# An attention and highway kernel: single PSUM banks for the first batches, paired output halves copied after both are written, x pairs of batches 3 and 4 moved ahead

## The chip, the cores and the metric

The kernel runs on one core of one Trainium2 chip. The metric is the device time of one execution in microseconds (us). The span that a profile shows, from the first to the last instruction, is about 1.8 us shorter than that time (136.5 against 138.31). PE is TensorE, PEld its weight load, DVE VectorE, ACT ScalarE, POOL GpSimd, SP SyncE. L12 is line 12 of the kernel that was profiled, so the same statement has another line number in each kernel.

## The reference, cut to what matters

```python
# q, k, v: 8 batches, 8 heads, 576 tokens, 64 columns
q_s = softmax(q, axis=-1);  k_s = softmax(k, axis=2)      # k over the tokens
kv  = einsum('bhsd,bhse->bhde', k_s, v)
x   = einsum('bhsd,bhde->bhse', q_s, kv)                  # then heads side by side: 4608 x 512
H   = maximum(x @ w_h, 0);  T = sigmoid(x @ w_t + b_t)
out = T * H + (1 - T) * x
```

For each batch the kernel takes exp of q and k (ScalarE), scales q by its row sums (VectorE, GpSimd), transposes q and forms kv (TensorE), multiplies them to x ("x pair": two halves of the heads; the ninth block of 64 tokens goes to tiles of its own), and then runs four **gates** (x @ w_t, then tanh on ScalarE) and four **carries** (x @ w_h, then a VectorE product `dd`). A VectorE **blend** gives `g`, GpSimd adds x to part of it, and TensorE turns the result back into rows (`nat`), which ScalarE or VectorE copies out of PSUM (`o`).

## The kernel before: what the change touches

The kernel uses eight PSUM banks: it gives four to a ring (`ps_ht`: gates and carries), two together to one tile (`ps_2`), and one each to `ps_1` and `ps_nat`. The framework places the semaphores from the accesses to each tile.

```python
def two_banks(name, dt=FP32):
    return ps_2.tile([P, 2, 2048 // (4 if dt is FP32 else 2)], dt, tag="q2", name=name)

halves = {}
def held(name, dt=FP32):                      # the same two-bank tile for two users
    if name not in halves:
        halves[name] = two_banks(name, dt)
    return halves[name]

def warm_mid(n, t):                           # dummy matmuls that keep TensorE busy
    for _ in range(n):
        mm(t(), ident, wide, True, True)
# ... start of batch 0 and 1, in program order:
E(x_pair, 0, 0, "AA"), E(warm_up, 2), E(x_pair, 0, 1, "AV"), E(warm_up, 1), E(x_left, 0),
# ... exps of q of batch 1, casts of w_h (ScalarE)
E(gate, 0, 0), E(gate, 0, 1), E(gate, 0, 2, lambda: held("m0")[:, 0]),
E(warm_mid, 5, lambda: held("m0")[:, 1]),
E(carry, 0, 0), E(blend, 0, 0), E(carry, 0, 1), E(exp_half, 1, "k", 0), E(gate, 0, 3, ...),
# ...
def out_tile(g, n, spare=False):
    # ... spare: the last group; n % 4 of 0 and 1 are the halves of one two-bank tile
    if spare and n % 2:
        nc.vector.tensor_copy(o, flat(t))
    else:
        nc.scalar.copy(o, flat(t))
```

The third gate and the dummies thus share one tile, in two banks of it. "AA" and "AV" say which engine copies each half of an x pair.

The softmax here doesn't subtract the row's maximum and nothing guards it: scores larger than these inputs give would overflow.

## Time and profile before

| | before |
|---|---|
| time, us: three runs first, four with the one beside the changed kernel | 136.55, 136.56, 136.75, 138.16 |
| profiled execution: time, span, mean clock | 138.31, 136.5, 0.967 |
| busy share of the span: PE, DVE, ACT, POOL | 85%, 73%, 68%, 51% |
| last v cast of batch 1 ends, ACT (us of the span) | 33.12 |
| TensorE's closed stretch (matmuls without a gap, 41.09 of 41.20 us busy) | 76.8 to 118.0 |

The page of the profile cuts the span into 40 slices of 3.41 us, and gives the busy share of each in tenths. Two of its rows:

```profile
PE   4939968798589879777998899999999999989950
PEclk9996896899999999999999999999999999999996
```

TensorE is closed from the 24th slice to the 35th. The second row is its granted clock. It is below 9 in the fourth, fifth, seventh and eighth slice: in this execution the clock was halved twice in the start. The profiled execution was thus among the slower ones of its kernel (138.31 against 136.55).

### The profile page before, as it was taken

To read this page: it belongs to the slowest core of one execution; us is meant where nothing else is said; L and a number is where in the kernel's file an instruction comes from. 1 tells how busy PE (TensorE), PEld (TensorE's weight loads), DVE (VectorE), ACT (ScalarE), POOL (GpSimd) and SP (SyncE) were. 2 spreads that over 40 slices of the span, in tenths; PEclk is the share of its full clock that TensorE was granted. 3 is DMA by queue.
4 is the path that set the end of the run, shared out by engine and by line. 5 is a ranking of instruction groups with operands and counts; after the bars stand their busy time and mean duration, and the time that the engine had idled before them with its cause. 6 is when DMAs were issued, how large, how long until landed. Compare 5 with 4: busy or idle time off the path is not lost.

```text
span 136.5 us, 3464 instructions
## 1 busy us (share of the span) xinstructions
PE 116.0 (85%) x1427; PEld 65.0 (48%) x1427; DVE 99.3 (73%) x180; ACT 92.6 (68%) x129; POOL 69.5 (51%) x64
## 2 busy tenths in 40 slices
PE   4939968798589879777998899999999999989950
PEld 1414413246135435533564465565466445678830
DVE  1386138159899999886699588988998656778760
ACT  3542059919689579736997989998995566665430
POOL 2005423780129999909951993399199704500000
PEclk9996896899999999999999999999999999999996
DMA  4999999999999999970699999995015007076754
GB/s 134 362 379 387 411 404 410 411 410 410 411 406 411 406 407 411 417 270 6 218 271 411 406 311 339 403 427 225 0 77 235 0 5 307 0 305 264 310 204 154
DMA packets 15847, 40.06 MB, mean 293 GB/s; under 512 B 724, under 2 KB 1240, under 8 KB 14808
## 3 DMA queue, kind: packets, MB, share of 16 engines
q1 hardware_dynamic: 15832, 39.85, 75.8%
q8 instruction: 11, 0.18, 0.5%
q14 instruction: 4, 0.03, 0.1%
HBM read 30.41 MB, written 9.44 MB: 292 GB/s over the span
## 4 chain that ended last, share of the span: by engine, by line
PE 61%; DVE 18%; ACT 11%; DMA 3%; issue 3%; SPq 0%; DVEq 0%; ACTq 0%
PE pt L63 18%; PE ph L63 17%; PE nat L63 8%; PE pq L68 5%; DVE dd L380 4%; PE psk L63 4%; ACT xT L333 4%; DMA q<-in_q_dram 3%; PE warm L63 3%; DVE g L388 3%; PE px L63 3%; ACT o L432 2%; DVE r L230 2%; DVE qsT L278 2%; ACT xT L336 2%
## 5 line engine op out<-in xcount | busy, mean ns | idle before, releaser
L260 POOL TENSOR_TENSOR eq<-eq,r 128x1024 f16<-128x1024 f16 (+2 forms) x16 | 29.7, 1876 | 20.6 <-DVE r L248 17.3
L63 PE MATMUL pt<-xT,w16t 128*128 128x512 f16 x124 | 34.0, 390 | 2.4 <-ACT xT L333 1.0
L362 ACT ACTIVATE pt<-pt,bt 128x512 f32<-128x512 f32 (+1 forms) x39 | 24.1, 621 | 16.9 <-PE pt L63 16.9
L63 PE MATMUL ph<-xT,w16h 128*128 128x512 f16 x128 | 32.8, 380 | 0.0
L380 DVE SCALAR_TENSOR_TENSOR dd<-xT,ph 128x512 f16<-128x512 f16 x32 | 21.8, 682 | 11.6 <-PE ph L63 9.6
L388 DVE SCALAR_TENSOR_TENSOR g<-pt,dd 128x512 f16<-128x512 f32 (+1 forms) x39 | 24.4, 627 | 2.7
L397 POOL TENSOR_TENSOR g<-g,xT 128x512 f16<-128x512 f16 x18 | 20.5, 1155 | 8.6 <-DVE g L388 8.6
L63 PEld LDWEIGHTS <-w16t 128*128 128x128 f16 x160 | 14.9, 100 | 18.0 <-issue 7.5
L181 ACT ACTIVATE eq<-q 128x1152 f16<-128x1152 f32 x16 | 18.6, 1174 | 2.8 <-DMA q<-in_q_dram 2.8
L181 ACT ACTIVATE ek<-k 128x1152 f16<-128x1152 f32 x16 | 18.5, 1169 | 1.7 <-DMA k<-in_k_dram 1.7
L230 DVE TENSOR_REDUCE r<-eq 128x18 f32<-128x1152 f16 x12 | 16.1, 1344 | 4.1 <-ACT eq L181 4.1
L193 POOL CAST v<-v 128x1152 f16<-128x1152 f32 x12 | 13.5, 1150 | 10.4 <-DMA v<-in_v_dram 10.4
L432 ACT COPY o<-nat 128x512 f32<-128x512 f32 x28 | 16.8, 598 | 2.8 <-PE nat L63 1.8
L63 PE MATMUL nat<-ident,g 128*128 128x128 f16 x142 | 17.8, 219 | 0.9 <-ACT o L432 0.6
L63 PEld LDWEIGHTS <-w16h 128*128 128x128 f16 x160 | 13.8, 98 | 9.8 <-issue 0.5
L63 PEld LDWEIGHTS <-g 128*128 128x128 f16 x144 | 13.7, 97 | 8.7 <-issue 2.4
L68 PE MATMUL pq<-ident,eq 128*128 128x128 f16 x134 | 11.1, 219 | 5.1 <-DVE qsT L278 2.7
L333 ACT CAST xT<-px 128x1024 f16<-128x1024 f32 x11 | 11.2, 1016 | 4.4 <-PE px L63 3.4
L68 PEld LDWEIGHTS <-eq 128*128 128x128 f16 x144 | 9.4, 98 | 9.6 <-issue 4.5
L63 PE MATMUL warm<-wide,ident 128*128 128x512 f16 x37 | 12.1, 472 | 1.8 <-DVE wide L152 1.8
L278 DVE COPY qsT<-pq 128x1024 f16<-128x1024 f16 (+1 forms) x22 | 12.3, 561 | 1.2 <-PE pq L68 0.6
L63 PE MATMUL nat<-ident,xT 128*128 128x128 f16 x56 | 9.7, 219 | 0.0
(55 smaller groups left out, 102.5 us busy)
## 6 DMA issues: line engine op xcount, KB each, us to landing
out_dram<-o SPq DMA_DIRECT2D x8, 1024.0 KB, 5.2
q<-in_q_dram SPq DMA_DIRECT2D x7, 1152.0 KB, 13.5
k<-in_k_dram SPq DMA_DIRECT2D x7, 1152.0 KB, 13.8
v<-in_v_dram SPq DMA_DIRECT2D x5, 1152.0 KB, 13.7
v<-in_v_dram SPq DMA_DIRECT2D x6, 576.0 KB, 11.6
q<-in_q_dram SPq DMA_DIRECT2D x2, 576.0 KB, 4.1
k<-in_k_dram SPq DMA_DIRECT2D x2, 576.0 KB, 7.3
w32t<-in_moe_w_t_dram SPq DMA_DIRECT2D x1, 1024.0 KB, 11.3
```

Source lines behind the costliest of these rows:

```text
L63: mm = lambda o, l, r, st, sp: nc.tensor.matmul(o, l, r, start=st, stop=sp, skip_group_check=True)
L68: nc.tensor.matmul(o, i, ident, is_transpose=True, start=True, stop=True, skip_group_check=True,)
L181: nc.scalar.activation(dst[b][:, :, 2 * a : 2 * a + 2, :], in32[which][b][:, 2 * a : 2 * a + 2].rearrange("p c n d -> p n c d"), AF.Exp,)
L230: nc.vector.reduce_sum(qsum[b][:, :, h], eq[b][:, :, h, :], axis=AX.X)
L260: nc.gpsimd.tensor_mul(e, e, r.broadcast_to(list(e.shape)))
L278: nc.vector.tensor_copy(qsT[b][:, :, n0:n1, :], t[:, :, 0:w, :])
L333: copy[how](dst, t2.rearrange("p c (n d) -> p c n d", d=64))
L362: nc.scalar.activation(ps, ps, AF.Tanh, bias=bt2[:, ob : ob + 1], scale=0.5)
L380: nc.vector.scalar_tensor_tensor(dd, xv(ob), -0.5, ps, op0=ALU.mult, op1=ALU.max)
L388: nc.vector.scalar_tensor_tensor(gv(ob), th, 1.0, dd, op0=ALU.add, op1=ALU.mult)
L397: nc.gpsimd.tensor_add(gv(ob), gv(ob), xv(ob))
L432: nc.scalar.copy(o, flat(t))
```

## The change

Its intent: TensorE should no longer wait for the reader of one bank before it writes another. So the second x pair of batch 0 goes to two single banks, the ninth tokens of batches 0 to 2 to single banks of two or three pools with one small copy each, and the dummies to a bank of their own. At the end each pair of output halves is written first and copied after. In batches 2 to 4 the order of transposes, kv and x pairs is moved by fractions of a step. The third group of q transposes of batch 0 gets a bank of its own too; this is left out of the cut below.

```diff
-    def warm_mid(n, t):
+    def warm_mid(n):
+        t = single("warm_mid")
         for _ in range(n):
-            mm(t(), ident, wide, True, True)
+            mm(t, ident, wide, True, True)
 ...
     def x_left(b):
-        t = two_banks(f"px_{b}_l").rearrange("p c (a w) -> p c a w", a=2)[:, :, :, 0:64]
         for c in range(2):
-            x9_mm(t, b, c)
-        x9_copy(t, b)
+            name = f"px_{b}_l{c}"
+            t = single(name) if c == 0 else two_banks(name)[:, 0] if b == 1 else nat_bank(name)
+            ... # four small matmuls
+            x9_copy(b, t, slice(c, c + 1))
 ...
-        if spare and n % 2:
+        if spare and n % 4 == 0:
+            pass
+        elif spare and n % 4 == 1:
+            nc.scalar.copy(o32[g, n // 4][:, 0, :], o32["2"][:, 0])
+            nc.vector.tensor_copy(o, o32["2"][:, 1])
+        elif spare and n % 2:
 ... # tile9: ps_1 and ps_nat in place of two halves of one two-bank tile
-            2: ((5, 6, 6.4), (4, 6.2), (7, 7.5)),
-            3: ((4, 5, 5), (4, 4), (6, 7)),
-            4: ((2, 3, 4), (5, 5), (6, 7)),
+            2: ((5, 6, 6.9), (4, 6.2), (7, 7.5)),
+            3: ((3.5, 4.9, 5.1), (4, 4), (5.9, 6.9)),
+            4: ((2, 3, 4), (4.5, 4.5), (5.9, 6.9)),
 ...
-        E(warm_up, 20),
+        E(warm_up, 24),
-        ... E(x_pair, 0, 1, "AV"), ...
+        ... E(x_pair, 0, 1, "AV", False, True), ...
-        ... E(gate, 0, 2, lambda: held("m0")[:, 0]), E(warm_mid, 5, lambda: held("m0")[:, 1]),
+        ... E(gate, 0, 2, lambda: two_banks("pt_0_2")[:, 0]), E(warm_mid, 5),
```

More of the change, by code (lines that the diff above doesn't have):

```diff
@@ L160, in two_banks @@
         return ps_2.tile([P, 2, 2048 // (4 if dt is FP32 else 2)], dt, tag="q2", name=name)
-    halves = {}
-    def held(name, dt=FP32):
-        if name not in halves:
-            halves[name] = two_banks(name, dt)
-        return halves[name]
-    def warm_mid(n, t):
+    single = lambda name: ps_1.tile([P, 512], FP32, tag="q1", name=name)
+    nat_bank = lambda name, dt=FP32: ps_nat.tile(
+        [P, 512 if dt is FP32 else 1024], dt, tag="nat", name=name
+    )
+    def warm_mid(n):
+        t = single("warm_mid")
         for _ in range(n):
-            mm(t(), ident, wide, True, True)
+            mm(t, ident, wide, True, True)
     ek, eq, psk, qsT = {}, {}, {}, {}
@@ L291, in x9_mm, with x9_copy @@
                 x_mm(t[:, c, a, :], b, a, c, x, NM, N9)
-    def x9_copy(t, b):
+    def x9_copy(b, t, c=slice(0, 2)):
         x9v = x9.rearrange("p (a c) b d -> p c a b d", c=2)
-        nc.vector.tensor_copy(x9v[:, :, :, b, :], t[:, :, :, 0:64])
+        nc.vector.tensor_copy(x9v[:, c, :, b, :], t)
     def x_left(b):
-        t = two_banks(f"px_{b}_l").rearrange("p c (a w) -> p c a w", a=2)[:, :, :, 0:64]
         for c in range(2):
-            x9_mm(t, b, c)
-        x9_copy(t, b)
+            name = f"px_{b}_l{c}"
+            t = single(name) if c == 0 else two_banks(name)[:, 0] if b == 1 else nat_bank(name)
+            t = t[:, 0:128].rearrange("p (z a w) -> p z a w", z=1, a=2)
+            for a in range(2):
+                for x in range(2):
+                    x_mm(t[:, 0, a, :], b, a, c, x, NM, N9)
+            x9_copy(b, t, slice(c, c + 1))
     x9t = {}
@@ L337, in x_pair @@
         if left and a == 1:
-            x9_copy(x9t[b], b)
+            x9_copy(b, x9t[b])
     rows_of = lambda c: 8 if c < B else 4
@@ L446, in tile9 @@
             o32["9", g // 2] = og.tile([P, 4, 512], FP32, tag="o32", name=f"o9_{g}")
-            o32["2"] = two_banks(f"nat9_{g}")
-        t = o32["2"][:, g % 2].rearrange("p (k d) -> p k d", k=4)
+        ps, tag = ((ps_1, "q1"), (ps_nat, "nat"))[g % 2]
+        t = ps.tile([P, 4, P], FP32, tag=tag, name=f"nat9_{g}")
         for k_ in range(nk):
@@ L551 @@
         E(exp_half, 0, "k", 1), E(cast_v, 0, 1),
-        E(q_trans, 0, 0), E(q_trans, 0, 1, lambda: held("q0", FP16)[:, 0]), E(warm_up, 2), E(q_trans, 0, 2, lambda: held("q0", FP16)[:, 1]),
+        E(q_trans, 0, 0), E(q_trans, 0, 1, lambda: two_banks("pq_0_1", FP16)[:, 0]), E(warm_up, 2), E(q_trans, 0, 2, lambda: nat_bank("pq_0_2", FP16)),
         E(warm_up, 6),
@@ L556 @@
         E(warm_up, 4),
-        E(x_pair, 0, 0, "AA"), E(warm_up, 2), E(x_pair, 0, 1, "AV"), E(warm_up, 1), E(x_left, 0),
+        E(x_pair, 0, 0, "AA"), E(warm_up, 2), E(x_pair, 0, 1, "AV", False, True), E(warm_up, 1), E(x_left, 0),
         E(exp_half, 1, "q", 0), E(q_sums_tree, 1, 0),
@@ L561 @@
         E(q_scale_p, 1, 0, 4), E(q_scale_p, 1, 4, 8),
-        E(gate, 0, 0), E(gate, 0, 1), E(gate, 0, 2, lambda: held("m0")[:, 0]), E(warm_mid, 5, lambda: held("m0")[:, 1]),
+        E(gate, 0, 0), E(gate, 0, 1), E(gate, 0, 2, lambda: two_banks("pt_0_2")[:, 0]), E(warm_mid, 5),
         E(carry, 0, 0), E(blend, 0, 0), E(carry, 0, 1), E(exp_half, 1, "k", 0),
-        E(gate, 0, 3, lambda: ps_nat.tile([P, 512], FP32, tag="nat", name="pt_0_3")), E(blend, 0, 1), E(carry, 0, 2),
+        E(gate, 0, 3, lambda: nat_bank("pt_0_3")), E(blend, 0, 1), E(carry, 0, 2),
         E(q_trans, 1, 0), E(blend, 0, 2), E(carry_products, 0, 3),
```

## The prediction

> **What bounds the kernel now.** I first read the busy shares of the page: TensorE 85%, VectorE 73%, ScalarE 68%. An average over stages says little, so I cut the span at the visible joints of the timeline and asked for the busy time of each engine in each stretch (columns: stretch, its length, then busy us and instructions of TensorE, weight load, VectorE, ScalarE, GpSimd, granted clock, DMA share, GB/s).
>
> ```profile
> 10.00:17.50 7.50, 7.19 (x105) 3.36 (x105) 3.31 (x8) 1.16 (x1) 3.47 (x4) 0.77 1.03 400
> 17.50:28.50 11.00, 8.48 (x42) 3.38 (x42) 4.38 (x11) 8.72 (x13) 5.73 (x7) 0.84 1.04 409
> 28.50:35.00 6.50, 5.60 (x110) 3.27 (x112) 5.91 (x12) 3.94 (x5) 2.29 (x4) 1.00 1.04 412
> 35.00:48.00 13.00, 11.13 (x146) 5.22 (x147) 12.15 (x25) 10.24 (x14) 7.94 (x8) 1.00 1.04 408
> 48.00:64.50 16.50, 12.76 (x177) 7.10 (x173) 14.52 (x24) 11.56 (x16) 13.21 (x10) 1.00 0.78 306
> 64.50:76.80 12.30, 11.31 (x165) 6.42 (x163) 10.28 (x17) 11.24 (x15) 7.85 (x7) 1.00 0.86 309
> 76.80:118.00 41.20, 41.09 (x538) 23.31 (x536) 32.87 (x54) 33.40 (x48) 27.24 (x21) 1.00 0.55 210
> 118.00:127.00 9.00, 8.29 (x96) 7.18 (x94) 7.21 (x15) 5.12 (x12) 0.94 (x1) 1.00 0.56 234
> ```
>
> From 76.8 to 118 us TensorE is busy 41.09 of 41.20 us: nothing in the change can shorten that. From 28.5 to 64.5 VectorE is nearly full (5.91 of 6.50, 12.15 of 13.00, 14.52 of 16.50): that work is a fixed train, and it ends earlier only if it starts earlier. So there are three places to win: the start up to about 33 us, the end after 118 us, and TensorE's holes at 48 to 76.8 us (3.7 and 1.0 us). The list of TensorE's waits (us in total, times, longest) shows what holes the change aims at.
>
> ```profile
> PE pq L68 <- DVE qsT L278: 2.7, 4, 1.8
> ...
> PE px_l L63 <- DVE xT L336: 1.1, 1, 1.1
> ...
> PE px L63 <- ACT xT L333: 0.9, 2, 0.5
> PE px_l L63 <- ACT xT L333: 0.9, 1, 0.9
> PE nat L63 <- ACT o L455: 0.9, 2, 0.6
> PE m L63 <- ACT m L362: 0.8, 1, 0.8
> ...
> PE nat L63 <- ACT o L432: 0.6, 2, 0.3
> ```
>
> The `m` line is the telling one: a dummy matmul into the second bank of the two-bank tile `m` waits for ScalarE's tanh in its first bank. The `nat` lines are the same thing in the output: the second half isn't written before the first is copied. These waits are between halves of one tile, not between bytes in use. Then the timeline of ScalarE and of TensorE in the start (start, us, engine, instruction, idle before and releaser):
>
> ```profile
> 19.57 0.59 ACT L336 CAST xT<-px 128x512 f16<-128x512 f32 x1 [0.51 <-PE px L63]
> ...
> 25.67 0.66 ACT L362 ACTIVATE m<-m,bt 128x512 f32<-128x512 f32 x1 [0.19 <-ACT pt L362]
> 26.26 1.15 ACT L181 ACTIVATE ek<-k 128x1152 f16<-128x1152 f32 x1
> 30.25 0.66 ACT L362 ACTIVATE pt<-pt,bt 128x512 f32<-128x512 f32 x1 [2.84 <-PE pt L63]
> ...
> 31.89 1.23 ACT L199 CAST v<-v 128x576 f16<-128x576 f32 x2
> ```
> ```profile
> 20.94 0.26 PE L63 MATMUL px_l<-qsT,kvn 64*64 64x64 f16 x8 [1.09 <-DVE xT L336]
> ...
> 26.38 1.24 PE L63 MATMUL m<-wide,ident 128*128 128x512 f16 x5 [0.80 <-ACT m L362]
> ```
>
> ScalarE idles 0.51 + 0.19 + 2.84 = 3.54 us between 17.99 (first x copy) and 33.12 (last v cast of batch 1, for which batch 1's kv product waits; it starts at 33.34). The 2.84 us end when TensorE delivers the fourth gate of batch 0, and TensorE is late because of its own waits above.
>
> **What the Trainium skill says.** "PSUM — Partial Sum Buffer", section "PSUM bank collisions raise a hardware error": engines have to be kept apart within one bank and quadrant of partitions; on different banks accesses run clean. So a wait between two banks is bookkeeping per tile, and a change of tile can remove it; the `m` wait of 0.80 us agrees. "Perfetto Trace Analysis", section "Matmuls": independent groups should rotate through different banks so that the copies of one overlap the next; the 41.09 of 41.20 us show this kernel doing it in its middle. "TensorE: Matmul & The Clock Gate", section "Part 1: The HAM clock gate": the clock halves after an idle window of about 3.4 us and returns after a busy one. The trace agrees: 0.77 and 0.84 granted at 10 to 28.5 us; 8 gate matmuls in 3.06 us there against 4 in 0.86 us of the chain of waits later.
>
> **The change part by part.**
>
> *Start.* Batch 0's second x pair goes to two single banks, its ninth tokens to two more, and the dummies to a third. Counting from the unchanged first pair at 17.53: the second pair follows two dummies at about 18.3 instead of 19.12; ScalarE's third copy joins the first two (19.06 to 19.65); VectorE's copy no longer waits behind ScalarE's (it did, at 20.19) and ends near 19.5. The ninth tokens don't wait, and the gates start near 19.1 to 19.7 instead of 21.13. TensorE then has work through the window in which it now idles, so the 12 gate matmuls should run warm (12 x 0.22 = 2.6 us, ending near 22.3 instead of 25.5), and the 5 dummies follow without the 0.80 us wait. TensorE is then ahead of ScalarE, and ScalarE's own work sets the pace without its holes: exp of q 2.2 (to 21.85), weight casts 2.17 (to 24.0; the last weight block leaves GpSimd at 22.33, so data is there), three tanh at 0.62 (to 25.9), exp of k 1.1, fourth tanh 0.62, exp of k 1.1, two v casts at 0.62: 29.95 instead of 33.12. **3.2 us.** VectorE's train before it (first product 28.52 to second q copy 33.98, 5.46 us) can start once the first carry is done at about 24.3, ending near 29.8, so it isn't later.
>
> *Warm-ups.* Four more at 0.22 us end near 8.5, before the first transposes at 10.03: they cost nothing. If they hold the clock over 11.5 to 14.9 us, kv of batch 0 starts up to 1 us sooner (the second v cast ends at 14.16, kv begins at 15.05), but weight blocks arriving until 22.3 us swallow part. I count 0; at best 1 us. The split of q0 removes no wait by itself: its copy ends at 12.24 and the dummies before the transposes at about 12.27.
>
> *Ninth tokens in two copies.* One 128x256 copy of 0.36 to 0.42 us becomes two 128x128 ones (the last copy of the kernel, 0.28 us, is of this size): about +0.15 us each for batches 1 and 2, inside VectorE's full stretch. **-0.3 us.** The 0.90 us wait of batch 2's ninth tokens goes, but the gate behind it needs the x copies ending at 49.5 anyway.
>
> *Batches 3 and 4.* Replayed by hand with the trace's durations. Batch 3: the first transposes move ahead of a gate and now wait for GpSimd's scaling (53.6, hole 0.6 us); the second q copy still stands behind kv norm and a 1.34 us sum on VectorE, so the third transpose stays near 58.8 (the 1.80 us hole becomes about 1.4). The first x pair gets to 59.6 instead of 60.4, its copy overtakes a tanh and an output copy on ScalarE, the second pair runs at 61.2 instead of 62.3, the copy ends at 63.3 instead of 63.8: 0.5 us. Batch 4: kv is earlier but its norm waits for a sum on VectorE, then two x copies of 1.0, a tanh 0.66 and an output copy 0.6 in a row on ScalarE: 0.2 us. **0.7 us.**
>
> *End.* TensorE's holes of 0.44 us before the second output halves (two of them, 120.33 and 123.63) and before the second ninth-token tile (127.98), and 0.61 at 130.95, go. But both copies now follow both writes, and VectorE's behind ScalarE's on the same two-bank tile: VectorE starts at 121.47 instead of 121.30, and then its train of 1.46 us per pair (copy 0.60, dd 0.51, g 0.35) is the bound, ending 0.2 us earlier at 126. After that single banks let both go: 0.6 by the last carry, 0.95 at the last copy. **0.95 us.**
>
> Sum: 3.2 - 0.3 + 0.7 + 0.95 = 4.55 us; 136.56 - 4.5 = **132.1 us**.
>
> **Rivals.**
> 1. *Data arrives too late.* The DMA share is full up to 58 us. If batch 2's q or v aren't there 3 us sooner, the gain of the start shrinks. Against: ScalarE shows only 2.8 us of waits for q in all, at the very start, and q of batch 2 isn't waited for at 33.02. For: GpSimd waits 4.2 us before its v cast at 34.49, probably a load. With 1.5 us lost: 133.6.
> 2. *The start's gain was already half there.* The profiled execution took 138.31, two of the three unprofiled ones 136.55 and 136.56. If those ran with the clock held, the start gains nearer 2 us: 133.3.
> 3. *The clock holds over 10 to 25 us with the extra dummies*: 131.1.
> 4. *Reordering backfires*: transposes that wait for GpSimd's scaling, or a fuller ScalarE in batches 3 and 4, cost 0.5 instead of gaining 0.7: 133.3.
>
> **Range and chances.** Rivals 1, 2 and 4 pull up, 3 pulls down; two at once rarely exceed 134.5. The line for 2% faster is 133.83, 1.7 us above my number: 0.80. Within 2%: 0.18. Slower would need the start to fail and the reordering to cost: 0.02.
>
> **What would show it.** Start right: no wait of px_l or of the dummies, gates before 20 us, kv of batch 1 near 30 us with ScalarE unbroken before it. Wrong if ScalarE still has a hole over 1 us there or waits for DMA. Middle right: the stretch that is now 76.8 to 118 begins 3 to 4 us sooner and is as long. Wrong if TensorE shows new holes there, behind GpSimd's eq or VectorE's qsT. End right: the last carry to the end is shorter, no nat wait on o; wrong if VectorE's copies make TensorE wait for banks.

## The result, and the profile after

The changed kernel takes 132.38 us in the median of four runs (132.09 to 132.51), before 136.66 us (136.55 to 138.16). The ratio of the fast runs is 0.966, with a 95% interval of 0.9591 to 0.9728: faster. A ratio here is always the mean time of one kernel's fast runs over that of the other's of the same rounds, so it isn't quite the ratio of the medians. The prediction was 132.1 us.

The same two rows of the page, for the changed kernel (slices of 3.25 us):

```profile
PE   4999997984988798599989999999999999999940
PEclk9999999999999999999999999999999999999999
```

In this execution (132.09 us) the clock was not halved again, but for the last 0.2 us, once it was whole (from 7.17 us by the trace's clock records; the row prints 9 before that too), while in the profiled execution of before it was, twice. Of the 6.3 us between the two spans (136.5 to 130.2) some 1.7 us are thus likely a difference of executions (138.31 against 136.55 for the kernel before); the timed runs, which show 4.3 us, decide.

ScalarE in the start (start, us, engine, instruction, in brackets the idle time before and what ended it):

```profile
16.00 1.56 ACT L339 CAST xT<-px 128x512 f16<-128x512 f32 x3 [5.04 <-PE px L63]
19.04 2.22 ACT L180 ACTIVATE eq<-q 128x1152 f16<-128x1152 f32 x2 [1.48 <-DMA q<-in_q_dram]
...
23.24 1.80 ACT L365 ACTIVATE pt<-pt,bt 128x512 f32<-128x512 f32 x3
24.95 1.17 ACT L180 ACTIVATE ek<-k 128x1152 f16<-128x1152 f32 x1
26.01 0.66 ACT L365 ACTIVATE pt<-pt,bt 128x512 f32<-128x512 f32 x1
26.58 1.17 ACT L180 ACTIVATE ek<-k 128x1152 f16<-128x1152 f32 x1
27.63 1.25 ACT L198 CAST v<-v 128x576 f16<-128x576 f32 x2
30.12 1.16 ACT L180 ACTIVATE eq<-q 128x1152 f16<-128x1152 f32 x1 [1.23 <-DMA q<-in_q_dram]
```

The four tanh, the two exps and the v casts follow each other without a hole; the last cast ends at 28.88 instead of 33.12. There are two new holes, both for loads. Exp of batch 1's q waits 1.48 us, so of the 2.0 us by which the first x pair comes sooner (17.53 to 15.53) only 1.0 us reaches ScalarE (20.06 to 19.04); exp of batch 2's q waits 1.23 us. The chain that ended last now runs through these two loads up to 30.12 us (14.32 and 10.99 us of it): loads of q are 19% of it, before 3%. TensorE in the same stretch:

```profile
17.27 2.76 PE L63 MATMUL pt<-xT,w16t 128*128 128x512 f16 x12
19.87 1.24 PE L63 MATMUL warm_mid<-wide,ident 128*128 128x512 f16 x5
21.83 0.39 PE L63 MATMUL ph<-xT,w16h 128*128 128x512 f16 x1 [0.72 <-ACT w16h L115]
```

Gates and dummies have no wait left, and the gates begin at 17.27 instead of 21.13. The first carry waits for the weight casts alone. The stretches of the changed kernel, to be laid beside the prediction's table (in order: length, then busy us and instructions of PE, PEld, DVE, ACT, POOL, then clock, DMA share, GB/s):

```profile
43.60:59.70 16.10, 12.92 (x179) 6.97 (x172) 14.29 (x25) 11.57 (x15) 12.79 (x10) 1.00 1.04 408
59.70:71.64 11.94, 11.39 (x166) 6.49 (x164) 10.46 (x18) 11.21 (x15) 8.05 (x6) 1.00 0.90 321
71.64:112.85 41.21, 41.11 (x539) 23.34 (x536) 33.31 (x55) 33.42 (x48) 27.71 (x22) 1.00 0.56 214
112.85:122.00 9.15, 9.01 (x107) 8.03 (x105) 7.48 (x16) 5.59 (x13) 0.94 (x1) 1.00 0.55 229
```

The closed stretch is 41.21 us long, as before, and begins 5.1 us sooner. After it TensorE is busy 9.01 of 9.15 us, where it had been busy 8.29 of 9.00.

The same events of the two profiled executions, in us of each span:

| event | before | after | sooner by |
|---|---|---|---|
| first x pair of batch 0, PE | 17.53 | 15.53 | 2.0 |
| last v cast of batch 1 ends, ACT | 33.12 | 28.88 | 4.2 |
| x copies of batch 1 begin, ACT | 35.36 | 31.19 | 4.2 |
| first x pair of batch 2, PE | 47.42 | 43.30 | 4.1 |
| output tile behind the first gate of batch 4 begins, PE | 76.78 | 71.64 | 5.1 |
| last 512-wide `dd`, DVE | 118.28 | 113.13 | 5.2 |
| end | 136.5 | 130.2 | 6.3 |

### The profile page after: what moved, and what is told of

Read it like the earlier page. It is cut to its first block, busy times and chain, and to the rows that moved or that the text cites. A ratio compares the mean times of both kernels' runs of the same rounds, so it can differ in the third digit from the quotient of the medians.

```text
span 130.2 us, 3470 instructions
## 1 busy us (share of the span) xinstructions
PE 114.8 (88%) x1431; PEld 64.5 (50%) x1431; DVE 99.8 (77%) x183; ACT 92.3 (71%) x129; POOL 70.5 (54%) x64
## 4 chain that ended last, share of the span: by engine, by line
PE 47%; DMA 19%; DVE 14%; POOL 9%; SPq 3%; issue 2%; ACT 2%; DVEq 0%; POOLq 0%
DMA q<-in_q_dram 19%; PE pt L63 17%; PE ph L63 15%; PE nat L63 6%; POOL eq L259 3%; PE pq L68 3%; DVE dd L383 3%; POOL g L400 3%; DVE g L391 2%; PE px L63 2%; PE psk L63 2%; SPq L95 2%; DVE r L229 2%; POOL v L192 2%; DVE xT L339 1%
## 5 line engine op out<-in xcount | busy, mean ns | idle before, releaser
L63 PE MATMUL ph<-xT,w16h 128*128 128x512 f16 x128 | 33.3, 380 | 1.1 <-ACT w16h L115 0.7
L365 ACT ACTIVATE pt<-pt,bt 128x512 f32<-128x512 f32 (+1 forms) x40 | 24.7, 622 | 12.0 <-PE pt L63 11.2
L391 DVE SCALAR_TENSOR_TENSOR g<-pt,dd 128x512 f16<-128x512 f32 (+1 forms) x40 | 25.0, 628 | 3.1 <-DVE dd L383 0.5
L63 PEld LDWEIGHTS <-w16h 128*128 128x128 f16 x160 | 13.7, 98 | 11.3 <-ACT w16h L115 2.5
L440 ACT COPY o<-nat 128x512 f32<-128x512 f32 x26 | 15.6, 600 | 0.1
L68 PE MATMUL pq<-ident,eq 128*128 128x128 f16 x144 | 12.0, 219 | 2.8 <-DVE qsT L277 2.1
L63 PE MATMUL warm<-wide,ident 128*128 128x512 f16 x41 | 12.6, 456 | 1.8 <-DVE wide L152 1.8
L277 DVE COPY qsT<-pq 128x1024 f16<-128x1024 f16 (+1 forms) x24 | 13.2, 553 | 1.1 <-PE pq L68 0.6
```

The source lines that it names most:

```text
L63: mm = lambda o, l, r, st, sp: nc.tensor.matmul(o, l, r, start=st, stop=sp, skip_group_check=True)
L68: nc.tensor.matmul(o, i, ident, is_transpose=True, start=True, stop=True, skip_group_check=True,)
L277: nc.vector.tensor_copy(qsT[b][:, :, n0:n1, :], t[:, :, 0:w, :])
L365: nc.scalar.activation(ps, ps, AF.Tanh, bias=bt2[:, ob : ob + 1], scale=0.5)
L391: nc.vector.scalar_tensor_tensor(gv(ob), th, 1.0, dd, op0=ALU.add, op1=ALU.mult)
```

## The experiments

The theory after the traces: three things gain, the dummies' own bank, the order in batches 3 and 4, and the end. The rivals: the 24 dummies hold the clock and that is most of it; or the other single banks of the start matter as much; or the later gains are hidden.

All twelve kernels gave correct results. Each was run six times (the profile and five rounds), beside eleven runs of the kernel before on the same chip. The twelve ran in three jobs of four, each on a chip of its own, so ratios from different jobs are from different chips too. The fast runs' means of the kernel before are 137.23 us beside the first four kernels, 137.32 for the next four and 137.67 for the last four. In eight of the twelve kernels one to four of the six executions fell more than 1.5% above the fastest; no time is compared with those, but some profiles are of such an execution.

### The clock: 24 dummies on the kernel before, 20 on the changed one

```diff
 # b_w24: the kernel before
-        E(warm_up, 20),
+        E(warm_up, 24),
 # a_w20: the changed kernel
-        E(warm_up, 24),
+        E(warm_up, 20),
```

> The kernel before with 24 dummies in place of 20 and nothing else. Theory (waits): the start was late because ScalarE stood still for TensorE (holes of 0.51 and 2.84 us), and the dummies only hold the clock; the first x pair may come 2 us sooner, but the dummies behind the third gate still wait for its tanh, which waits for the weight casts, so the first carry comes at 25.5 to 26.5 us instead of 27.46 and the time falls by 0 to 1.2 us, to 135.4 to 136.7. Rival (clock): the held clock is most of the start's gain; then 133.5 to 134.5.

> The changed kernel with 20 dummies at its start. Waits: the clock drops at about 11.5 us, kv of batch 0 is late by 1 to 2 us, but the weight blocks that arrive until 22 us hide half of it: 132.6 to 133.6. Clock: it falls back by 2 us or more, 134.5 to 135.5.

The kernel before with 24 dummies has a ratio of 1.0064 (1.0003 to 1.0125), all six executions fast: no gain. The changed kernel with 20 has 0.9619 (0.9548 to 0.9689), with two fast executions, 131.73 and 132.39 us, which lie on those of the changed kernel (132.10 to 132.68 in the run `a_again` below). The count of dummies at the very start isn't what made the kernel faster. The rival falls; so does my own guess that 20 would cost 0.2 us or more, as far as two fast executions can say. Executions with the same mean clock agree: in the job of `a_again` the changed kernel took 132.10 us at 0.975, the kernel before 136.73 us at 0.977.

The profile of the kernel before with 24 dummies shows that they don't surely hold the clock. Two stretches of it, one window of 3.41 us each:

```profile
7.85:11.26 3.41, 1.55 (x18) 0.91 (x17) 3.27 (x7) 2.33 (x2) 0.00 (x0) 1.00 1.03 399
11.26:14.67 3.41, 3.41 (x14) 1.36 (x12) 1.16 (x3) 0.00 (x0) 2.29 (x2) 0.50 1.02 388
```

TensorE was busy 1.55 us of the first window, and the clock was halved for the whole of the next. In another kernel, with the same 24 dummies, the window lay 0.12 us later (7.97 to 11.38), TensorE was busy 1.67 us in it, and the clock stayed whole.

### The start taken apart: the dummies' bank, and the other banks

```diff
 # a_oldmid: the changed kernel, dummies back in the second bank of the third gate's tile
-    E(gate, 0, 2, lambda: two_banks("pt_0_2")[:, 0]), E(warm_mid, 5),
+    E(gate, 0, 2, lambda: held("m0")[:, 0]), E(warm_mid, 5, lambda: held("m0")[:, 1]),
 # a_oldpair: the changed kernel, batch 0's second x pair and ninth tokens back in two-bank tiles
-    E(x_pair, 0, 1, "AV", False, True),
+    E(x_pair, 0, 1, "AV"),
     def x_left(b):
+        if b == 0:  ... # one two-bank tile, one copy, as before
```

> The changed kernel with the five dummies back in the second bank of the third gate's tile, nothing else undone. Waits: they wait again for the third tanh, which ends at 25.0 us in the changed kernel, so the first carry ends near 27 instead of 23.8 us and ScalarE gets a hole of 2 to 3 us before the fourth gate's tanh: 134.4 to 135.2. Rival (this wait is hidden, as the weight casts until 23.3 us hold the carry anyway): 132.2 to 132.9.

> The changed kernel with batch 0's second x pair and its ninth tokens back in two-bank tiles. The waits return (second pair 0.5 to 0.7 us, ninth tokens about 1.1 us), so the gates start 1.4 to 2 us later, near 19 us. If only what holds the carry counts (the weight casts, ending at 23.3 us), all of it is hidden: 132.1 to 132.8. If the gates' start is on the path: 133.6 to 134.5.

With the dummies' wait put back the ratio is 0.9928 (0.9877 to 0.9979): 135.57 to 137.05 us, so of the gain 3.5 us are gone between the fastest executions (135.57 against 132.10 of `a_again`) and 4.0 us by the ratios (0.9928 against 0.9635, of 137.3 us), more than I expected. Its profile, first TensorE, then ScalarE:

```profile
24.13 1.44 PE L63 MATMUL m<-wide,ident 128*128 128x512 f16 x5 [3.93 <-ACT m L371]
25.37 3.42 PE L63 MATMUL ph<-xT,w16h 128*128 128x512 f16 x8
```
```profile
29.68 0.66 ACT L371 ACTIVATE pt<-pt,bt 128x512 f32<-128x512 f32 x1 [4.53 <-PE pt L63]
```

The same edit that in the kernel before cost a wait of 0.80 us costs 3.93 us here. The gates now end sooner, but the tanh for which the dummies wait still stands behind ScalarE's weight casts, so what TensorE gains it waits. And the dummies, which are there to keep the clock, come too late: TensorE was busy 0.90 us in the window before 25.03, and the next 3.42 us ran at half clock, so that the first two carries took 3.42 us, against 1.89 in the kernel before. ScalarE then waits 4.53 us for the fourth gate.

With the other banks put back the ratio is 0.9648 (0.9581 to 0.9715); its four fast executions are 131.97, 131.98, 132.10 and 133.81 us. Waits of 0.64 and 1.09 us return on TensorE in its profile (a slow execution, from which I take only that), and cost nothing that the fast runs show. The carries are held by the weight casts anyway, and these stand behind exp of batch 1's q, for whose load the changed kernel waited 1.48 us.

### The dummies' bank alone, and no dummies

```diff
 # b_mid: the kernel before
-    def warm_mid(n, t):
+    def warm_mid(n):
+        t = ps_1.tile([P, 512], FP32, tag="q1", name="warm_mid")
 # a_nomid: the changed kernel
-    E(gate, 0, 2, ...), E(warm_mid, 5),
+    E(gate, 0, 2, ...),
```

> The kernel before with one edit: the five dummies behind the third gate get a single bank of their own. If this wait is the start's whole gain (undoing it in the changed kernel cost 3.5 us, from 132.1 to 135.6 in the fastest runs): 3 us faster than before, 133.4 to 134.0 in its fastest runs against 136.4 to 136.7. Rival (it needs the other single banks too, since before's gates start 2 us later): 1 to 1.5 us, 135.0 to 135.6.

> The changed kernel without the five dummies. If the harm was the wait alone, the dummies are worth little, since TensorE stood only about 2.3 us idle in their place: 132.0 to 132.8. Rival (an idle window of 2 to 3 us there drops the clock for the carries, as the 3.9 us wait did when the dummies were put back): slower by 1 us or more in most executions, 133.2 to 134.5.

The one edit on the kernel before gives 0.984 (0.9762 to 0.9918); the three fast executions are 135.03, 135.23 and 135.96 us, 2.3 us under the mean of before (137.67). The fastest ones lie in the range of the rival (135.0 to 135.6). It is not the whole 3.5 to 4.0 us: in the profile of this kernel (a slow execution) the gates begin at 21.14 us, as before, and a hole of 1.88 us stays before the fourth tanh. The rival's reason, the other single banks, isn't shown: putting them back in the changed kernel lost nothing. What the edit is worth depends on when the gates come, so worths found in the two kernels can't be added.

Without any dummies the ratio is 0.9642 (0.9557 to 0.9728), with three fast executions (131.82, 132.47, 133.76 us). So the fast ones lose at most little, and the harm was the wait. Three executions were slow; whether the missing dummies make that more frequent, six runs can't say.

### The order in batches 2 to 4, and the end

```diff
 # a_again: the changed kernel once more
 # a_oldorder: the changed kernel with the three rows of positions of the kernel before
 # a_oldend: the changed kernel with the old end
-        if spare and n % 4 == 0: ... # both halves copied after both are written
+        if spare and n % 2:          # each half copied when it is written
-        ps, tag = ((ps_1, "q1"), (ps_nat, "nat"))[g % 2]
+        o32["2"] = two_banks(...)    # ninth-token tiles as halves of one tile
```

> The changed kernel again, as the measure for the runs beside it: 132.1 to 132.6.

> The changed kernel with the old order of transposes, kv and x pairs in batches 2 to 4. If the reordering is worth what I predicted (0.7 us) or what the two traces suggest (1.0 us between 43 and 72 us): 133.0 to 133.5. Rival (VectorE and GpSimd carry those batches, the order on TensorE is hidden): 132.2 to 132.6, within 0.2 us of the changed kernel beside it.

> The changed kernel with the old end: half one copied before half two is written, ninth-token tiles in the halves of one two-bank tile. Predicted worth 0.95 us, the traces say 1.2 us: 133.2 to 133.7. Rival (the holes of TensorE only move, since VectorE's train bounds the end): under 0.5 us, 132.3 to 132.9.

The changed kernel had 0.9635 (0.9561 to 0.9709) this time, fast executions 132.10 to 132.68 us. The old order had 0.9704 (0.9647 to 0.9761): five executions from 133.40 to 133.74 us and one of 132.28. The difference of the ratios is 0.0069 of 137.3 us, 0.9 us. The reordering is worth about what the traces said. TensorE's waits at 49 to 73 us, old order first, then the changed kernel of the same job:

```profile
PE pq L68 <- DVE qsT L277: 1.8, 1, 1.8
PE pt L63 <- ACT xT L336: 1.0, 2, 0.5
PE px L63 <- ACT xT L336: 0.9, 2, 0.5
```
```profile
PE pq L68 <- DVE qsT L277: 1.2, 1, 1.2
PE px_l L63 <- DVE qsT L277: 0.5, 1, 0.5
PE px_l L63 <- DVE kvn L219: 0.5, 1, 0.5
PE pq L68 <- POOL eq L259: 0.4, 1, 0.4
```

3.7 us of waits become 2.6. The waits for the copies of the x pairs are gone; new ones on VectorE and GpSimd stand in their place, but they are smaller.

The old end had 0.9754 (0.9692 to 0.9816), all six executions fast, 133.08 to 134.91 us: 0.0119 of 137.3 us, 1.6 us by the means, and 1.0 us between the fastest executions (133.08 against 132.10). The rival of under 0.5 us falls. In its profile TensorE waits again four times for a ScalarE copy, 0.9 us in two and 0.6 us in two, as in the kernel before; in the changed kernel there is no such wait.

### One copy for the ninth tokens of batches 1 and 2

```diff
 # a_x9one: the changed kernel
     def x_left(b):
+        if b > 0:  ... # one two-bank tile, one copy, as before
```

> The changed kernel with the ninth tokens of batches 1 and 2 in one two-bank tile and one copy each. I predicted that two copies cost VectorE 0.3 us in all: then 131.9 to 132.2, 0.3 us faster. Rival (the small copies overlap, two of them took 0.42 to 0.48 us together against 0.36 to 0.42 us for the one): within 0.1 us; and if batch 2's wait of 0.9 us for the two-bank tile comes back on the path, slower by 0.2 us or more.

The ratio is 0.9676 (0.9604 to 0.9748). The fast executions fall in two groups, 132.01 and 132.07, and 133.14 to 133.77, while those of the changed kernel lie between. This is inconclusive: a term of 0.3 us can't be seen under such scatter.

### Two edits against what the changed kernel now waits for

```diff
 # a_q2half: the changed kernel, batch 2's q in two transfers
-        *[E(load, 2, w) for w in "qk"], ...
+        E(load, 2, "q", [nc.sync, nc.sync]), E(load, 2, "k"), ...
 # a_best: this, and at the end one ScalarE copy for both halves of a two-bank tile
-            nc.scalar.copy(o32[g, n // 4][:, 0, :], o32["2"][:, 0])
-            nc.vector.tensor_copy(o, o32["2"][:, 1])
+            nc.scalar.copy(o32[g, n // 4][:, 0:2, :], o32["2"])
```

> The changed kernel with batch 2's q loaded in two halves, so that the first exp needs only the first. In the changed kernel ScalarE waits 1.23 us for that load before 30.12 us. If that is on the path: the wait falls below 0.3 us and the time by 0.4 to 0.7 us, to 131.5 to 132.0 in the fastest runs. Rival (GpSimd, held until 34.7 us by the load of v, sets when the scaling of batch 2's q starts): within 0.2 us, 131.9 to 132.5.

> Batch 2's q in two halves, and at the end both halves of a two-bank output tile in one ScalarE copy (about 1.0 us) in place of one copy on each engine in series. If VectorE's train bounds the end (it has no hole over 0.1 us from 116.37 to 125.8 us), taking two copies of 0.6 us from it gains 0.4 to 0.8 us more than the halves alone: 130.9 to 131.6 in the fastest runs. Rival (ScalarE's longer copy delays the tanh that VectorE and TensorE need next): no better than the halves alone.

Two halves remove the 1.23 us wait: exp of batch 2's q starts at 28.86 in its profile, directly behind the v casts. The ratio is 0.9626 (0.9564 to 0.9687), the fast executions 131.99 to 133.34 us: nothing that the runs show. As the rival had it, GpSimd's next v cast waits for its load until 34.74, and the scaling of q begins at 35.62 instead of 36.03.

With the single copy at the end the ratio is 0.9533 (0.9475 to 0.959), five fast executions of 130.76 to 131.61 us and one slow one. This is 1.4 us under the changed kernel by the ratios (0.9635 - 0.9533 = 0.0102, of 137.5 us), and its slowest fast execution lies below the fastest of the changed kernel. It beats both kernels. VectorE at the end of the changed kernel, and ScalarE at the end of this one:

```profile
115.42 0.42 DVE L391 SCALAR_TENSOR_TENSOR g<-pt,dd 128x256 f16<-128x256 f32 x1 [0.48 <-DVE dd L383]
116.37 0.69 DVE L436 COPY o<-nat 128x512 f32<-128x512 f32 x1 [0.53 <-ACT o L435]
```
```profile
115.22 1.02 ACT L435 COPY o<-nat 128x1024 f32<-128x1024 f32 x1
```

In the changed kernel VectorE waits 0.53 us for ScalarE's copy of the other bank of the same tile and then has no listed hole until 0.27 us before its last copy. One copy of 1.02 us takes both 0.69 us copies from it. `a_q2half` ran in the same job and differs by this copy alone: 1.3 us by the ratios (0.9626 - 0.9533 = 0.0093, of 137.67 us), 1.2 us between the fastest executions (131.99 and 130.76), and the fast executions of the two don't overlap. So the copy is nearly all of it. Their profiles show about 0.75 us of this in the end: from the last 512-wide `dd` to the end of the span 17.4 us (112.74 to 130.1) became 16.6 us (112.60 to 129.2). The rest is not accounted for.

## Why the prediction was right

**The bound.** Right. The closed stretch kept its 41.2 us to a hundredth, so the gains before it arrived at the end in full: 5.1 us at its start, 5.2 us at its end. That its start moved by more than the 3 to 4 us of the prediction's sign is likely the slower execution that was profiled before.

**The start, 3.2 us through ScalarE's unbroken work.** The mechanism was right. From exp of batch 1's q to the last v cast ScalarE took 13.06 us before (20.06 to 33.12) and takes 9.84 us now (19.04 to 28.88), 3.2 us less, since the holes of 0.19 and 2.84 us went. The step was shown by putting the dummies' wait back, which opened a hole of 4.53 us and cost 3.5 to 4.0 us. One of the prediction's own signs of being wrong came up all the same: ScalarE waited 1.48 us for a load, that of batch 1's q. The working let exp of q begin at 19.65, with an unchanged first pair at 17.53. The first pair came at 15.53, and the load let 1.0 us of this through, so the wait only cut a gain that the working hadn't counted. Two sizes were off. The prediction spread the gain over second pair, ninth tokens, dummies and clock, as if each wait counted; in the changed kernel's surroundings the first two are worth nothing that the fast runs show, and the dummies' wait, for which it named 0.80 us, is worth 3.5 to 4.0 us there and 2.3 us in the kernel before. And the wait is no constant: it is the distance from the end of the gates to a tanh that the weight casts hold, so it grows as the gates come sooner.

**The warm-ups.** Counting 0 was right. Whether they help to hold the clock is open: in the eleven profiles of the changed kernel and its variants it was not halved before 19.9 us, in one with 20 dummies (`a_w20`, a slow execution) neither; in the three of the kernel before and its variants it was halved at 11.3 to 11.5 us, in one with 24 (`b_w24`) too. Neither timed comparison showed a gain.

**Ninth tokens, -0.3 us.** Not settled. The traces say that the term was too large: from the start of the copy to the start of the next VectorE instruction it is 0.28 us for the one copy of batch 1 (39.99 to 40.27) and 0.33 us for the two (35.80 to 36.13), and 0.33 (49.42 to 49.75) and 0.40 us (45.29 to 45.69) for batch 2, so the two copies cost 0.12 us in all, as the second copy begins before the first ends. The timed run can't resolve it.

**Batches 3 and 4, 0.7 us.** Right in mechanism and nearly in size: 1.0 us in the traces (from 4.1 us at the first x pair of batch 2 to 5.1 us at 71.64), 0.9 us by the run with the old order. Both sides of the working show: the new wait for GpSimd's scaling (0.4 us), which the prediction had named as a sign of being wrong, and the shortened one for VectorE (1.8 to 1.2 us), which is worth more.

**The end, 0.95 us.** Right: 1.15 us in the traces (118.28 to 136.50 against 113.13 to 130.20), 1.2 us between those of `a_oldend` and `a_again` (113.73 to 132.0 against 113.80 to 130.8), 1.0 us between fastest runs, 1.6 us by means. VectorE's copy did wait behind ScalarE's, and VectorE had no hole after it, as worked out; the run with one copy for both shows that this was what was left to gain.

**Rival 1, data too late,** was partly there: q of batch 1 was waited for 1.48 us and q of batch 2 1.23 us, and the 4.7 us by which batch 1's x pair was sooner (34.90 to 30.19) shrank to 4.2 us at its copies. Taking the wait for batch 2's q away alone gained nothing measurable, since the load of v holds GpSimd just behind it. **Rival 2** was right as far as it said that the profiled execution of before was slow: subtracting the traces gives 6.3 us, and the runs 4.3 us. The sum of 4.55 us escaped this because its terms were worked out from waits, with the warm-ups counted as 0, and laid on the median of the runs.

**The total** of 4.5 us came out at 4.3 us. The parts undone one by one give 3.5 to 4.0, 0.9 and 1.0 to 1.6 us, 5.4 us or more, above the 4.9 us of the job of `a_again` (137.32 against 132.46). With the dummies' bank as measured on the kernel before (2.3 us) in place of the first they give 4.2 to 4.8 us. So the parts depend on each other, and the good total doesn't prove each size.

**What the Trainium skill adds.** "Perfetto Trace Analysis", section "Optimizing Scalar/DVE Operations", advises to group operations into larger ones on an engine that is full, and to give work to ScalarE where VectorE is full. The last run agrees: one 128x1024 copy took 1.02 us on ScalarE against 0.59 us for 128x512, it took work from the engine that was full, and that kernel was the fastest.

## What to carry to other kernels

Look for waits between the banks of one tile: if a dummy or a second half waits for the reader of the first, give it a tile of its own, and ask not how long it waits today but what it would wait for when everything ahead of it is sooner. Filler that is meant to keep the clock must not depend on anything that can be late, or it idles TensorE just before the work it should have warmed; and try leaving it out, which here lost little if anything in the fast runs. And before subtracting two traces, compare each profiled execution's time with the other runs of its kernel.

## What the Trainium skill lacked or had wrong

- "TensorE: Matmul & The Clock Gate", section "Part 1: The HAM clock gate", has the clock halved after an idle window of about 3.4 us and gives as the rule no idle gaps of more than that. Here it was halved for 3.41 us after windows in which TensorE was busy 0.90, 1.20, 1.55 and 1.69 of 3.41 us. In the last of them, 18.31 to 21.72 us of the kernel before, the longest wait was 1.09 us, and in the changed kernel run again TensorE was busy 1.56 us from 29.19 to 32.60, with no wait over 0.99 us, and the next 3.42 us ran at half clock. A window with 1.67 us busy left it whole (7.97 to 11.38 us of the changed kernel with the old dummies). Cut at the clock's own steps of 3.41 us, as the traces record them, the fourteen profiles (five of slow executions) have 497 such windows at the whole clock. It was halved after all 20 in which TensorE was busy 1.56 us or less, after none of the 459 with 1.88 us or more, and after ten of the 18 between (1.61 to 1.72 us). So a share of busy time near a half tells the two apart, and no idle gap of 3.4 us is needed; the small 64-row matmuls and the transposes may count otherwise, which no run here separates.
- The same section says that the windows run freely, so that the start of the whole clock varies by 500 ns either way. The runs agree with the first, and the spread is larger: in the fourteen profiles the first matmul starts at 1.81 or 1.82 us of the span, and the clock is first recorded whole between 4.44 and 7.61 us. Executions of one kernel spread by 2 to 3 us (132.10 to 134.96 for the changed one in one job); that the windows' place is the cause of this isn't shown.
- No page has this: with the framework used here, two engines that read different banks of one PSUM tile were put one behind the other (VectorE 0.53 us behind ScalarE), and so were a writer of one bank and a reader of the other (0.80 and 3.93 us). In tiles of their own batch 0's second x copies (VectorE had waited 2.16 us for ScalarE at 20.19) and the dummies had no such wait.
